# State read of blocks 2 to 7: softmax columns turned by VectorE in 32x32 squares and spread over partitions by DMA, with the division by the sum behind the read

## The chip, the cores and the metric

The kernel runs on one core of one Trainium2 chip. The metric is the device time of one execution in microseconds (us); the median of three runs of the kernel before is 890.83 us. A core has five engines with instruction queues of their own: TensorE (PE; its weight loads are listed as PEld), VectorE (DVE), ScalarE (ACT), GpSimd (POOL) and SyncE (SP), which here issues the DMAs.

## The reference, cut to what matters

Shapes: B = 8 blocks (batches), H = 8 heads, S = 512 tokens, NS = 32 states, D = 64. The change lies in the second softmax, which lets the states read from the tokens.

```python
scores = scale * x @ state.T                 # [B, H, S, NS]
xread  = softmax(scores) @ state             # tokens read from the states
scores2 = scale * state @ x.T                # [B, H, NS, S]
a2 = exp(scores2 - scores2.max(-1))
a2 /= a2.sum(-1) + 1e-9
sread = a2 @ x                               # states read from the tokens
y = concat([xread, sread], axis=2)           # 576 rows of width 512 per block
y = y + relu(layernorm(y) * g @ w_ch1) @ w_ch2
out = (sigmoid(causal_conv(y)) * (y @ w_val)) @ w_out
```

## The kernel before, in words

The eight blocks are worked one after the other by `segment`, which runs over sixteen pieces f of the hidden layer. One piece is, on PE, six matmuls of 512 columns into a PSUM bank `mm` (L77 to L79, `mm<-ahl,m`) and, one piece later, twelve matmuls of 512 columns that add the hidden piece into four banks `acc` (`acc<-hid,w`). Between them ACT (L680) and DVE (L684) take the hidden piece out of `mm`, of which there are two banks.

The attention of block b+1 is done in the background of block b: `background(b)` yields once per piece, and in it `attention_steps(b + 1)` does a step at each yield: scores (L213), the two softmaxes, the turning of the second softmax (`softmax2_turn`, L287), and three yields later the state read (`sread`, L304). PE's order is the order of the program; the order on the other engines and on SP's queue is set by a scheduler from priorities. Block 2 differs: its attention runs in the second half of block 1 (pieces 8 to 15, after two quiet yields), which has too few yields, so that what is left of its steps stands together at piece 15.

The second softmax has two tiles `a2[u]` of 128 rows (4 heads x 32 states) by 512 tokens. The read needs the tokens on the partitions. So in `softmax2_norm` ACT divides `a2` by its sum (L279, two instructions of 128x512), in `softmax2_turn` PE turns it (eight transposes of 128x128, L287, against the identity) into two PSUM tiles `at`, ACT copies these into SBUF (L291, two of 128x512), and in `sread` PE does 32 small matmuls (L304; each is two records in the trace, so 64) of a 128x32 piece against the tokens `xn`. DVE turns the result in 32x32 squares (L308, 128x128) and SP stores it by four DMAs into `x1d` (L310).

Tiles with the tag `t2` share six buffers of 128x512. SP's DMAs signal their end on eight semaphores, DMAHW0 to DMAHW7, in turn: a DMA is issued only when the one eight places before it has landed.

Of the kernel before, what the change touches and what calls it, by code (L numbers as in the profile page):

```python
# [14 lines left out]
AF = mybir.ActivationFunctionType  # L15
# [5 lines left out]
P = 128  # L21
B, H, S, NS, D = 8, 8, 512, 32, 64
DM = H * D
DFF = 4 * DM
KT = DM // P
# [19 lines left out]
def tile_kernel(ctx: ExitStack, tc: tile.TileContext, xT, xk, stT, sn, w1, w2, wval, wout, convw, gln, ident, out):  # L45
    nc = tc.nc
# [8 lines left out]
    def sb(shape, dt, tag, bufs=1):  # L55
        cnt[0] += 1
        return main.tile(shape, dt, tag=tag, bufs=BUFS.get(tag, bufs), name=f"{tag}_{cnt[0]}")

    def ps(pool, tag, shape):
        cnt[0] += 1  # L60
        return pool.tile(shape, F32, tag=tag, name=f"{tag}_{cnt[0]}")

    def at_ps(shape):
        return ps(ps_at, "at", shape)

    def t2(shape):
        return sb(shape, F32, "t2")

    def small(shape, dt, tag):
        return sb(shape, dt, tag, 2)  # L70
# [10 lines left out]
    def at_prio(p):  # L81
        tc.cur_priority = p
# [14 lines left out]
    def load_state(b, eng=nc.sync):  # L97
        st_raw = small([P, KT, NS], F32, "st_raw")
        eng.dma_start(out=st_raw, in_=stT[b])
        sn_raw = small([P, 2, D], F32, "sn_raw")  # L100
        eng.dma_start(out=sn_raw, in_=sn[b])
        loads[b] = [st_raw, sn_raw]

    def load_x(b, eng=nc.sync):
        xt = sb([P, KT, S], F32, "big")
        eng.dma_start(out=xt, in_=xT[b])
        loads[b].append(xt)

    def load_xk(b):
        xn = sb([P, 4, H, D], F32, "big")  # L110
        nc.sync.dma_start(out=xn, in_=xk[b])
        loads[b].append(xn)

    def state_coefs(b):
        st_raw, sn_raw = loads[b][:2]
        stg = small([P, KT, NS], F32, "stg")
        eng = nc.vector if b == 1 else nc.gpsimd
        a = eng.tensor_tensor(stg, st_raw, g_sb.to_broadcast([P, KT, NS]), op=ALU.mult)
        if b == 1:
            behind(a, "dve")  # L120
        sbn = small([P, 2, 1], F32, "sbn")
        a = nc.vector.tensor_reduce(sbn.rearrange("p u o -> p (u o)"), sn_raw, axis=AX.X, op=ALU.add)
        if b == 1:
            behind(a, "dve")
        nc.vector.tensor_scalar(sbn, sbn, -1.0 / DM, None, op0=ALU.mult)
        sbhl = small([P, 2, 2, 1], F32R, "sbhl")
        split_sb(sbhl[:, 0], sbhl[:, 1], sbn, eng)
        coef[b] = (stg, sn_raw, sbn, sbhl)
# [79 lines left out]
    def scores(b, sc):  # L208
        st_raw, _, xt = loads[b][:3]
        for p in range(KT):  # L210
            for u in range(2):
                r = slice(64 * u, 64 * u + 64)
                nc.tensor.matmul(sc[u][32 * p:32 * p + 32, :], lhsT=st_raw[r, p, :], rhs=xt[r, p, :], start=True, stop=True)  # L213
        e1 = []
        for u in range(2):
            e = t2([P, 16, NS])
            nc.vector.transpose(e.rearrange("p g n -> p (g n)"), sc[u])
            e1.append(e)
        att[b] = e1

    def softmax1_max(b):
        e1 = att[b]
        mx = sb([P, 2, 16, 1], F32, "mxden")
        for u in range(2):
            nc.vector.tensor_reduce(mx[:, u].rearrange("p g o -> p (g o)"), e1[u], axis=AX.X, op=ALU.max)
            nc.vector.tensor_tensor(e1[u], e1[u], mx[:, u].to_broadcast([P, 16, NS]), op=ALU.subtract)
            nc.scalar.activation(e1[u], e1[u], AF.Exp, scale=SCALE)

    def softmax1_norm(b):
        e1 = att[b]  # L230
        den = sb([P, 2, 16, 1], F32, "mxden")
        for u in range(2):
            nc.vector.tensor_reduce(den[:, u].rearrange("p g o -> p (g o)"), e1[u], axis=AX.X, op=ALU.add)
        dv = den.rearrange("p u g o -> p (u g o)")
        nc.vector.tensor_scalar(dv, dv, 1e-9, None, op0=ALU.add)
        nc.vector.reciprocal(dv, dv)
        for u in range(2):
            nc.vector.tensor_tensor(e1[u], e1[u], den[:, u].to_broadcast([P, 16, NS]), op=ALU.mult)
# [14 lines left out]
    def softmax1_out(b):  # L253
        softmax1_turn(b)
        softmax1_split(b)

    a2s = {}

    def softmax2_exp(b, sc):
        if b:  # L260
            a2 = [t2([P, S]) for _ in range(2)]
        else:
            a = sb([P, KT, S], F32, "x1")
            a2 = [a[:, u] for u in range(2)]
        nmax = small([P, 2], F32, "nmax")
        sum2 = small([P, 2], F32, "sum2")
        for u in range(2):
            nc.vector.tensor_reduce(nmax[:, u:u + 1], sc[u], axis=AX.X, op=ALU.max)
            nc.scalar.activation(nmax[:, u:u + 1], nmax[:, u:u + 1], AF.Copy, scale=-SCALE)
            nc.scalar.activation(a2[u], sc[u], AF.Exp, bias=nmax[:, u:u + 1], scale=SCALE, accum_out=sum2[:, u:u + 1])  # L270
        a2s[b] = (a2, sum2)

    def softmax2_norm(b):
        a2, sum2 = a2s[b]
        r2 = small([P, 2], F32, "r2")
        nc.vector.tensor_scalar(r2, sum2, 1e-9, None, op0=ALU.add)
        nc.vector.reciprocal(r2, r2)
        for u in range(2):
            nc.scalar.activation(a2[u], a2[u], AF.Copy, scale=r2[:, u:u + 1])  # L279

    def softmax2_turn(b):
        a2 = a2s[b][0]
        a2T = []
        for u in range(2):
            tp = at_ps([P, 4, P])
            for c in range(4):
                nc.tensor.transpose(tp[:, c, :], a2[u][:, c * P:(c + 1) * P], ident_sb)  # L287
            t = t2([P, 4, P])
            p = tc.cur_priority
            at_prio(p - HLEAD)  # L290
            nc.scalar.copy(t, tp)  # L291
            at_prio(p)
            a2T.append(t)
        a2s[b] = a2T

    def sread(b):
        a2T = a2s.pop(b)
        xn = loads[b][3]
        sr = ps(ps_mm, "mm", [P, 2, D]) if b > 1 else at_ps([P, 2, D])
        for u in range(2):  # L300
            for c in range(4):
                for p in range(KT):
                    r = slice(32 * p, 32 * p + 32)
                    nc.tensor.matmul(  # L304
                        sr[r, u, :], lhsT=a2T[u][:, c, r], rhs=xn[:, c, 2 * p + u, :], start=(c == 0), stop=(c == 3)
                    )
        srs = t2([P, 4, 32])
        nc.vector.transpose(srs.rearrange("p t n -> p (t n)"), sr.rearrange("p u d -> p (u d)"))  # L308
        for p in range(KT):
            nc.sync.dma_start(  # L310
                out=x1d[b, :, p, :].rearrange("(t j) n -> j t n", j=32), in_=srs[32 * p:32 * p + 32]
            )
# [43 lines left out]
    def mean_terms(b):  # L356
        sbn, aT = coef[b][2], aTs[b]
        t = t2([P, S])
        nc.scalar.activation(t, aT[:, 0], AF.Copy, scale=sbn[:, 0])
        nc.vector.scalar_tensor_tensor(t, aT[:, 1], sbn[:, 1], t, op0=ALU.mult, op1=ALU.add)  # L360
        terms[b] = halves_of(t, S)
# [71 lines left out]
    def attention_steps(b):  # L433
        state_coefs(b)
        sc = [at_ps([P, S]) for _ in range(2)]
        scores(b, sc)
        softmax2_exp(b, sc)
        yield
        softmax1_max(b)
        yield  # L440
        softmax2_norm(b)
        yield
        softmax1_norm(b)
        yield
        softmax2_turn(b)
        yield
        softmax1_out(b)
        mean_terms(b)
        yield
        yield  # L450
        sread(b)
        yield
        if b + 1 < B:
            load_state(b + 1)
            load_x(b + 1)
            load_xk(b + 1)
# [436 lines left out]
    def first():  # L893
        x1 = x1_steps(0)
        next(x1)
        yield
        next(x1)
        state_coefs(1)
        yield
        yield  # L900
        softmax1_split(0)
        next(x1)
        yield
        att1 = attention_start(1)
        next(att1)
        yield
        softmax2_norm(0)
        next(att1)
        yield
        next(att1)  # L910
        for _ in x1:
            pass
        softmax2_turn(0)
        yield
        sread(0)
        yield
# [166 lines left out]
```

## Time and profile before

| what | value |
|---|---|
| median of 3 runs | 890.83 us (890.58 to 890.91) |
| the profiled execution: its own time / its span | 890.99 us / 889.2 us |
| busy: PE / DVE / ACT / POOL | 873.5 / 571.8 / 385.8 / 210.3 us |
[...]
| PE matmuls of L287, blocks 1 to 7 (56) | 7.5 us busy |
| PE matmuls of L304, blocks 2 to 7 (384 records) | 6.6 us busy |

Busy time is a sum over an engine's instructions, merged where they overlap. The span is what the profiler saw from the first to the last instruction; the execution's own time holds 1.8 us more around it.

### The profile page before, as it was taken

Reading aid. Unit: us, or ns where it says so; the run is one execution under the profiler, and the core shown is the slowest. Engines: PE = TensorE matmul, PEld = TensorE weight load, DVE = VectorE, ACT = ScalarE, POOL = GpSimd, SP = SyncE. Lnnn points to the kernel's source line nnn. Section 1 sums busy time; section 2 is a strip of 40 time slices with the busy share of each in tenths; the row PEclk is TensorE's granted clock in tenths of the full one; section 3 lists DMA queues with packets and bytes.
Section 4 is the critical chain, followed back from the end, with each engine's and each line's share of the span. In section 5 each row is a group of like instructions: output and inputs, shape, how many; then the busy total and the mean of one; then the engine's idle time right before and its main releaser. Section 6 shows DMA issues by size and latency. Waiting matters only on the chain.

```text
span 889.2 us, 12522 instructions
## 1 busy us (share of the span) xinstructions
PE 873.5 (98%) x4970; PEld 666.0 (75%) x4970; DVE 571.8 (64%) x957; ACT 385.8 (43%) x715; POOL 210.3 (24%) x172
## 2 busy tenths in 40 slices
PE   7997999999999999999999999999999999999998
PEld 2355767777777777777777777777899988888886
DVE  6899985666644553573464446243468799988870
ACT  4865744243433341443443235132337555455531
POOL 0001010013234321513522442162301124322100
PEclk8999999999999999999999999999999999999999
DMA  9932210121112101211120100110130212222112
GB/s 358 408 109 74 98 52 1 74 73 53 51 48 76 54 0 52 74 51 52 51 71 1 63 36 1 27 48 1 48 139 6 95 71 77 90 96 95 69 73 72
DMA packets 26667, 66.44 MB, mean 75 GB/s; under 512 B 10864, under 2 KB 13040, under 8 KB 22512
## 3 DMA queue, kind: packets, MB, share of 16 engines
q1 hardware_dynamic: 25984, 65.24, 20.4%
q8 instruction: 39, 0.64, 0.3%
q10 hardware_dynamic: 624, 0.40, 0.2%
q14 instruction: 20, 0.16, 0.1%
HBM read 47.80 MB, written 17.83 MB: 74 GB/s over the span
## 4 chain that ended last, share of the span: by engine, by line
PE 92%; DVE 4%; DMA 2%; ACT 1%; issue 1%; SPq 0%; DVEq 0%; ACTq 0%
PE acc L77 16%; PE acc L78 16%; PE acc L79 16%; PE mm L77 9%; PE mm L78 9%; PE mm L79 9%; PE at L144 2%; PE at L77 2%; PE at L79 2%; PE at L78 2%; PE mm L144 1%; PE mm L982 1%; DMA big<-in_xT 1%; PE mm L651 1%; PE acc L697 1%; PE at L287 1%
## 5 line engine op out<-in xcount | busy, mean ns | idle before, releaser
L77 PE MATMUL acc<-hid,w 128*128 128x512 f32 (+1 forms) x560 | 212.3, 379 | 0.1
L78 PE MATMUL acc<-hid,w 128*128 128x512 f32 (+1 forms) x560 | 211.4, 378 | 0.0
L79 PE MATMUL acc<-hid,w 128*128 128x512 f32 (+1 forms) x560 | 211.3, 377 | 0.0
L684 DVE SCALAR_TENSOR_TENSOR hid<-mm,hid 128x512 fp32r<-128x512 f32 (+1 forms) x140 | 91.8, 655 | 159.5 <-ACT hid L680 159.4
L680 ACT ACTIVATE hid<-mm 128x512 fp32r<-128x512 f32 (+2 forms) x144 | 82.2, 571 | 205.5 <-PE mm L79 204.1
L77 PE MATMUL mm<-ahl,m 128*128 128x512 f32 (+1 forms) x312 | 119.7, 384 | 3.4 <-DVE ahl L249 1.7
L77 PEld LDWEIGHTS acc<-hid,w 128*128 128x128 f32 x560 | 105.4, 188 | 23.0 <-issue 1.7
L79 PEld LDWEIGHTS acc<-hid,w 128*128 128x128 f32 x560 | 105.4, 188 | 19.8
L78 PEld LDWEIGHTS acc<-hid,w 128*128 128x128 f32 x560 | 105.4, 188 | 19.5
L78 PE MATMUL mm<-ahl,m 128*128 128x512 f32 (+1 forms) x312 | 115.3, 369 | 1.2 <-DVE m L74 1.2
L79 PE MATMUL mm<-ahl,m 128*128 128x512 f32 (+1 forms) x312 | 115.0, 369 | 0.0
L763 DVE SCALAR_TENSOR_TENSOR ahl<-big,cw,ahl 128x511 f32<-128x511 f32 (+3 forms) x128 | 102.2, 843 | 0.3
L74 POOL TENSOR_TENSOR m<-mb,m 128x512 fp32r<-128x512 f32 x48 | 61.4, 1299 | 123.0 <-ACT m L73 123.0
L73 ACT ACTIVATE m<-mb 128x512 fp32r<-128x512 f32 x62 | 38.7, 632 | 110.7 <-DVE mb L155 110.5
L77 PEld LDWEIGHTS mm<-ahl,m 128*128 128x128 f32 x312 | 58.8, 188 | 36.7 <-issue 12.1
L78 PEld LDWEIGHTS mm<-ahl,m 128*128 128x128 f32 x312 | 58.9, 189 | 11.3 <-DVE m L74 2.4
L79 PEld LDWEIGHTS mm<-ahl,m 128*128 128x128 f32 x312 | 58.8, 189 | 9.9
L749 POOL TENSOR_TENSOR w<-big,w 128x512 fp32r<-128x512 f32 x24 | 38.1, 1617 | 92.8 <-ACT w L747 92.8
L78 PE MATMUL acc<-w,raw 128*128 128x512 f32 (+1 forms) x144 | 54.3, 377 | 0.0
L79 PE MATMUL acc<-w,raw 128*128 128x512 f32 (+1 forms) x144 | 54.3, 377 | 0.0
L77 PE MATMUL acc<-w,raw 128*128 128x512 f32 (+1 forms) x144 | 54.3, 377 | 0.0
L711 DVE TENSOR_TENSOR t<-acc,t 128x512 f32<-128x512 f32 (+1 forms) x44 | 28.0, 660 | 28.3 <-PE acc L79 28.2
(183 smaller groups left out, 1294.9 us busy)
## 6 DMA issues: line engine op xcount, KB each, us to landing
w<-in_w SPq DMA_DIRECT2D x20, 512.0 KB, 8.6
big<-in_xT SPq DMA_DIRECT2D x8, 1024.0 KB, 5.1
big<-in_xk SPq DMA_DIRECT2D x8, 1024.0 KB, 5.3
x2d<-x SPq DMA_DIRECT2D x8, 1024.0 KB, 4.0
big<-x2d SPq DMA_DIRECT2D x8, 1024.0 KB, 4.9
out<-hid SPq DMA_DIRECT2D x16, 512.0 KB, 2.8
raw<-in_w SPq DMA_DIRECT2D x12, 512.0 KB, 6.7
raw<-in_wval SPq DMA_DIRECT2D x4, 512.0 KB, 4.1
```

What stands on the lines that cost most here:

```text
L73: nc.scalar.activation(hi, src, AF.Copy)
L74: eng.tensor_tensor(lo, src, hi.bitcast(F32), op=ALU.subtract)
L77: nc.tensor.matmul(acc, lhsT=wh, rhs=xl, start=first, stop=False)
L78: nc.tensor.matmul(acc, lhsT=wl, rhs=xh, start=False, stop=False)
L79: nc.tensor.matmul(acc, lhsT=wh, rhs=xh, start=False, stop=last)
L144: nc.tensor.matmul(mp[u][32 * p:32 * p + 32, :], lhsT=stg[r, p, :], rhs=w1s[4 * q + p][r], start=True, stop=True)
L287: nc.tensor.transpose(tp[:, c, :], a2[u][:, c * P:(c + 1) * P], ident_sb)
L680: marks["act"] = nc.scalar.activation(hid[:, 0], h, AF.Relu)
L684: marks["dve"] = nc.vector.scalar_tensor_tensor(hid[:, 1], h, 0.0, hid[:, 0].bitcast(F32), op0=ALU.max, op1=ALU.subtract)
L711: marks["dve"] = nc.vector.tensor_tensor(t, accs[d], rrow, op=ALU.mult)
L749: nc.gpsimd.tensor_tensor(lo, src, hi.bitcast(F32), op=ALU.subtract)
L763: t = nc.vector.scalar_tensor_tensor(g[:, j:], x[:, :n - j], cw_sb[:, k, PAD - j:TAPS - j], g[:, j:], op0=ALU.mult, op1=ALU.add)
```

## The change

For blocks 2 to 7 `softmax2_turn` gives way to `softmax2_spread`. DVE turns each 32x32 square of `a2[u]` in place of the whole (`nc.vector.transpose`, one instruction of 128x512 for each u), and sixteen DMAs for each u (32 rows of 512 bytes, 16 KB) move the squares to the partitions that they belong to. The tokens come out in another order over the partitions; the host lays `xk` out to suit for these blocks. The division by the sum moves behind the read for all eight blocks: ACT scales the 128x64 results (two instructions) out of PSUM into a tile `read`, and DVE turns that one. Blocks 0 and 1 keep the transposes on PE.

```diff
@@ softmax2_norm
-        for u in range(2):
-            nc.scalar.activation(a2[u], a2[u], AF.Copy, scale=r2[:, u:u + 1])
+        r2s[b] = r2
@@ softmax2_turn
-            a2T.append(t)
+            a2T.append(t.rearrange("p c (k n) -> p c k n", n=32))
+        a2s[b] = a2T
+
+    def softmax2_spread(b):
+        a2 = a2s[b][0]
+        a2T = []
+        for u in range(2):
+            turned = t2([P, 4, P])
+            nc.vector.transpose(turned.rearrange("p q x -> p (q x)"), a2[u])
+            t = t2([P, 4, P])
+            for p in range(KT):
+                for q in range(4):
+                    nc.sync.dma_start(out=t[32 * q:32 * q + 32, p], in_=turned[32 * p:32 * p + 32, q])
+            a2T.append(t.rearrange("p k (c n) -> p c k n", n=32))
         a2s[b] = a2T
@@ sread
-                        sr[r, u, :], lhsT=a2T[u][:, c, r], rhs=xn[:, c, 2 * p + u, :], start=(c == 0), stop=(c == 3)
+                        sr[r, u, :], lhsT=a2T[u][:, c, p], rhs=xn[:, c, 2 * p + u, :], start=(c == 0), stop=(c == 3)
-        srs = t2([P, 4, 32])
-        nc.vector.transpose(srs.rearrange("p t n -> p (t n)"), sr.rearrange("p u d -> p (u d)"))
+        read, srs, r2 = t2([P, 2, D]), t2([P, 4, 32]), r2s.pop(b)
+        for u in range(2):
+            nc.scalar.activation(read[:, u], sr[:, u], AF.Copy, scale=r2[:, u:u + 1])
+        nc.vector.transpose(srs.rearrange("p t n -> p (t n)"), read.rearrange("p u d -> p (u d)"))
@@ attention_steps
-        softmax2_turn(b)
+        softmax2_spread(b)
@@ kernel (host layout)
+    xk = x.reshape(B, H, 4, P, D).transpose(0, 3, 2, 1, 4).copy()
+    xk[2:] = x[2:].reshape(B - 2, H, 4, 4, 32, D).transpose(0, 2, 4, 3, 1, 5).reshape(B - 2, P, 4, H, D)
```

The first place is PE at the end of block 1's pieces, where block 2's turn and read stand. In the kernel before, eight transposes and six matmuls stand ahead of the read:

```order
L79 MATMUL acc_297_1541<-hid_1681,w_13_243_1226 128x512
L287 MATMUL at_1725<-ident_78,t_307_1589 128x128 x4
L287 MATMUL at_1732<-ident_78,t_308_1590 128x128 x4
L77 MATMUL mm_1739<-ahl_642,m_1510 128x512
L78 MATMUL mm_1739<-ahl_642,m_1510 128x512
L79 MATMUL mm_1739<-ahl_642,m_1510 128x512
L77 MATMUL mm_1739<-ahl_642,m_1510 128x512
L78 MATMUL mm_1739<-ahl_642,m_1510 128x512
L79 MATMUL mm_1739<-ahl_642,m_1510 128x512
L304 MATMUL mm_1761<-big_1178,t_328_1730 32x64 x16
L304 MATMUL mm_1761<-big_1178,t_330_1737 32x64 x16
```

In the changed kernel the transposes are gone from this row and the rest stands as it did. In blocks 3 to 7, too, only the transposes leave PE's order; there 54 matmuls of other work stand between turn and read.

The second place is VectorE ahead of block 2's read, behind the maxima of the first softmax (L225); here the changed kernel's row:

```order
L225 TENSOR_REDUCE mxden_1623<-t_308_1589 128x16
L698 SCALAR_TENSOR_TENSOR hid_1608<-mm_1601,hid_1608 128x512
L300 STREAM_TRANSPOSE t_329_1725<-t_309_1591 128x512
L226 TENSOR_TENSOR t_307_1587<-t_307_1587,mxden_1623 128x512
L226 TENSOR_TENSOR t_308_1589<-t_308_1589,mxden_1623 128x512
L276 TENSOR_SCALAR r_318_1652<-sum_312_1594 128x2
L300 STREAM_TRANSPOSE t_331_1744<-t_310_1592 128x512
L698 SCALAR_TENSOR_TENSOR hid_1637<-mm_1630,hid_1637 128x512
```

The two transposes (L300; L698 is the old L684) are new, before and behind the subtractions of L226; the scheduler has put them as soon as their exponentials are there, well ahead of where the step stands in the program. Blocks 3 to 7 have the same row. On SP's queue the 32 DMAs of block 2 then stand so:

```order
L730 DMA x2d_69<-x_71_328 128x2048
L106 DMA big_1831<-in_xT 128x2048
L99 DMA st_raw_2445<-in_stT 128x128
L304 DMA t_330_1727<-t_329_1725 32x128 x16
L304 DMA t_332_1746<-t_331_1744 32x128 x16
L111 DMA big_1833<-in_xk 128x2048
L324 DMA x1d<-t_341_1819 32x4x32 x4
```

They lie between the loads of the next block's `xT` and state and the load of its `xk`, which in both kernels waits for the read.

The third place is the read itself on PE in block 4, with the semaphores that each matmul waits for; the changed kernel's row:

```order
L316 MATMUL mm_3020<-big_2451,t_530_2903 32x64 [waits DMAHW3_49,DMAHW2_49,DMAHW6_49,DMAHW1_49,DMAHW0_49]
L316 MATMUL mm_3020<-big_2451,t_530_2903 32x64 [waits DMAHW6_49,DMAHW7_49,DMAHW5_49,DMAHW4_49]
L316 MATMUL mm_3020<-big_2451,t_530_2903 32x64 [waits DMAHW2_49,DMAHW3_49,DMAHW1_49,DMAHW0_49]
L316 MATMUL mm_3020<-big_2451,t_530_2903 32x64 [waits DMAHW6_49,DMAHW7_49,DMAHW5_49,DMAHW4_49]
L316 MATMUL mm_3020<-big_2451,t_530_2903 32x64 x12
L316 MATMUL mm_3020<-big_2451,t_532_2922 32x64 [waits DMAHW2_49,DMAHW3_49,DMAHW1_49,DMAHW0_49]
L316 MATMUL mm_3020<-big_2451,t_532_2922 32x64 [waits DMAHW6_49,DMAHW7_49,DMAHW5_49,DMAHW4_49]
L316 MATMUL mm_3020<-big_2451,t_532_2922 32x64 [waits DMAHW2_49,DMAHW3_49,DMAHW1_49,DMAHW0_49]
L316 MATMUL mm_3020<-big_2451,t_532_2922 32x64 [waits DMAHW6_49,DMAHW7_49,DMAHW5_49,DMAHW4_49]
L316 MATMUL mm_3020<-big_2451,t_532_2922 32x64 x12
```

The first four matmuls of each half u each wait for the four DMAs that filled their piece. Waits beyond what a matmul carries itself are instructions of their own on PE's queue: the built program has 16 of them in each read of blocks 3 to 7 and 17 in that of block 2, where the kernel before had at most one.

## Rows read from the trace of the kernel before

**Rows 1.** The page: busy time of each engine, share of the span, instructions.
```profile
PE 873.5 (98%) x4970; PEld 666.0 (75%) x4970; DVE 571.8 (64%) x957; ACT 385.8 (43%) x715; POOL 210.3 (24%) x172
```

**Rows 2.** The page: the chain that ended last, by engine.
```profile
PE 92%; DVE 4%; DMA 2%; ACT 1%; issue 1%; SPq 0%; DVEq 0%; ACTq 0%
```

**Rows 3.** Busy time by stretch: span; PE, PEld, DVE, ACT, POOL; clock; DMA.
```profile
236.00:274.00 38.00, 38.00 (x253) 29.73 (x253) 17.38 (x30) 12.72 (x24) 7.39 (x7) 1.00 0.10 30
```

**Rows 4.** PE's timeline (start, us, what), block 3's turn.
```profile
247.58 1.09 PE L287 MATMUL at<-ident,t 128*128 128x128 f32 x8
248.57 0.50 PE L77 MATMUL mm<-ahl,m 128*128 128x512 f32 x1
```

**Rows 5.** PE's timeline, block 2's turn and read.
```profile
192.07 0.39 PE L79 MATMUL acc<-hid,w 128*128 128x512 f32 x1
192.30 1.04 PE L287 MATMUL at<-ident,t 128*128 128x128 f32 x8
193.09 0.48 PE L77 MATMUL mm<-ahl,m 128*128 128x512 f32 x1
...
194.64 1.10 PE L304 MATMUL mm<-big,t 128*32 128x64 f32 x64
```

**Rows 6.** PE's timeline, block 3's read.
```profile
261.04 1.10 PE L304 MATMUL mm<-big,t 128*32 128x64 f32 x64
262.07 1.09 PE L144 MATMUL at<-w,stg 64*32 64x512 f32 x16
263.09 0.50 PE L77 MATMUL mm<-ahl,m 128*128 128x512 f32 x1
```

**Rows 7.** Line L304: durations in ns (min/median/max), first and last start.
```profile
L304 PE MATMUL mm<-big,t x384: 219/219/243, 194.6 to 563.7; 128*32 128x64 f32 x192
...
L304 PEldq EVENT_SEMAPHORE  x3: 51/51/51, 66.6 to 191.4; - x3
```

**Rows 8.** DVE's timeline in blocks 2 and 3; brackets: idle before, its releaser.
```profile
178.91 1.28 DVE L226 TENSOR_TENSOR t<-t,mxden 128x512 f32<-128x512 f32 x2
...
234.07 0.68 DVE L684 SCALAR_TENSOR_TENSOR hid<-mm,hid 128x512 fp32r<-128x512 f32 x1
...
262.21 0.32 DVE L308 STREAM_TRANSPOSE t<-mm 128x128 f32<-128x128 f32 x1 [2.46 <-PE mm L304]
```

**Rows 9.** DVE's groups: count, busy us, mean ns, idle before.
```profile
L243 DVE STREAM_TRANSPOSE aT<-t 128x512 f32<-128x512 f32 x16 | 10.5, 687 | 0.0
```

**Rows 10.** ACT's groups, likewise.
```profile
L279 ACT ACTIVATE t<-t,r 128x512 f32<-128x512 f32 x14 | 9.3, 711 | 0.0
L291 ACT COPY t<-at 128x512 f32<-128x512 f32 x16 | 9.0, 575 | 2.5 <-PE at L287 2.5
...
L680 ACT ACTIVATE hid<-mm 128x256 fp32r<-128x256 f32 x16 | 6.1, 379 | 18.3 <-PE mm L79 18.2
```

**Rows 11.** ACT's timeline behind block 3's read.
```profile
264.04 1.23 ACT L73 ACTIVATE m<-mb 128x512 fp32r<-128x512 f32 x2 [5.02 <-DVE mb L155]
```

**Rows 12.** SP's timeline: DMA issues of blocks 2, 4 and 7.
```profile
175.20 0.38 SPq L99 DMA_DIRECT2D st_raw<-in_stT  x1
...
338.06 1.81 SPq L310 DMA_DIRECT2D x1d<-t  x4
...
564.32 2.02 SPq L310 DMA_DIRECT2D x1d<-t  x4
```

**Rows 13.** Line L310, the 16 KB stores: issue in ns, landing in us.
```profile
L310 SPq DMA_DIRECT2D x1d<-t x32: 303/424/1631, 73.8 to 565.9; - x32
...
DMA to landing us min/median/max: 1.5/3.9/5.8
```

**Rows 14.** DMA issues of block 7's stores alone: KB, us to landing.
```profile
x1d<-t SPq DMA_DIRECT2D x4, 16.0 KB, 1.7
```

**Rows 15.** The chain that ended last, in block 0's turn: start, us, what.
```profile
65.88 0.65 DVE mb L155
66.53 0.60 DVE c L523
```

More of the change, by code (lines that the diff above doesn't have):

```diff
@@ L255, in softmax1_out @@
         softmax1_split(b)
-    a2s = {}
+    a2s, r2s = {}, {}
     def softmax2_exp(b, sc):
@@ L1059 @@
         "xT": x.reshape(B, KT, 2, S, D).transpose(0, 2, 4, 1, 3).reshape(B, P, KT, S),
-        "xk": x.reshape(B, H, 4, P, D).transpose(0, 3, 2, 1, 4),
+        "xk": xk,
         "stT": state.reshape(B, KT, 2, NS, D).transpose(0, 2, 4, 1, 3).reshape(B, P, KT, NS),
```

## The prediction

> **What bounds the kernel now.** I read the page first: PE is busy for 98% of the span [rows 1], and 92% of the chain that ended last lies on PE [rows 2]. The stretch that holds block 3's turn and read says the same from nearer: of 38 us, PE has 38.0, VectorE 17.4, ScalarE 12.7, at full granted clock and with the DMA engines a tenth busy [rows 3]. So what is taken from VectorE or ScalarE is worth nothing by itself, nor does adding to them cost anything while their results come in time. What counts is PE's time, and waits that open on PE. I then went to PE's timeline at the turn and the read, to the engines that feed them, and to SP's issues, since the change puts 192 DMAs there.
>
> **What it removes from PE.** In block 3 the eight transposes take from 247.58 to the start of the next L77 at 248.57, 0.99 us [rows 4]. Blocks 3 to 7 look alike, so five times 0.99 is 4.95. Block 2's take from 192.30 to 193.09, 0.79 [rows 5]. Together −5.74 us. (The table's 7.5 us for 56 such matmuls is busy time, which counts the overlap with neighbours; I take the starts.)
>
> **What it moves on ScalarE and VectorE.** ScalarE loses two divisions of 0.711 and two copies of 0.575 us in a block, 2.6 us, and gains two of 128x64. No row has that shape; 128x256 takes 0.379 [rows 10], and I estimate 0.23 for a quarter of the division's width. VectorE gains two transposes of 128x512, 0.687 each [rows 9], 1.4 us in a block. Both engines have over half of the 38 us free [rows 3], so I cost this at nothing. What could spoil it is the PSUM bank: VectorE released the read's bank at 262.21 + 0.32 = 262.53 [rows 8]; now ScalarE does, some 0.46 us behind the read's end at about 262.2, at 262.7. If the next L77 at 263.09 [rows 6] needs that bank, 0.4 us is still free, and ScalarE idles there (5.02 us before 264.04) [rows 11]. Without that idle time it would be up to 0.7 us (a division's length) in a block; I take 0. In blocks 0 and 1, where only the division moves, the chain runs over VectorE while ScalarE divides (65.88 to 67.1) [rows 15], so nothing is gained there; at most the two divisions, 1.4 us.
>
> **When the spread is done.** A DMA takes SP 424 ns to issue (303 to 1631) and lands 1.5 to 5.8 us after, median 3.9 [rows 13]. Four of them in a row take 1.81 us (0.45 apart) in block 4 and 2.02 in block 7 [rows 12]. The 3.9 is that of stores queued right behind a load of 1 MB; block 7's, which have none ahead, landed in 1.7 [rows 14], and the spread has none close ahead, so it is nearest to those. These go to DRAM, the new ones from SBUF to SBUF, which no row shows. I take 0.46 apart and 1.7 to land: 31 × 0.46 + 1.7 = 16.0 us from the first issue to the last landing. The bounds are 31 × 0.35 + 1.5 = 12.4 (0.35 an estimate inside the issue's 303 to 424 ns) and 31 × 0.53 + 3.9 = 20.3.
>
> In block 3 the last exponential's neighbour on VectorE, L684 at 234.07, ends at 234.75 [rows 8]; with a transpose behind it the first DMA goes at about 235.4 and the last lands at 251.4, at the latest bound 255.7. The read is due at 261.04 [rows 6] less the 0.99, at 260.05. So 8.6 us are free, and the wait costs nothing in blocks 3 to 7 unless issues come (24.6 − 1.7)/31 = 0.74 us apart. Behind the spread on SP stand the load of the next tokens and the stores, which wait for the read anyway.
>
> Block 2 has no such room. Its first transpose takes the place of the subtraction at 178.91 [rows 8] and ends at 179.6; SP has been free since 175.58 [rows 12]. The second ends before SP is through the first sixteen. The last landing is at 179.6 + 16.0 = 195.6 (192.0 to 199.9). The read starts at 194.64 [rows 5], less 0.79, and its second half, whose DMAs are last, half a microsecond later: 194.36. PE then waits 1.2 us, and nothing else can go, since its order is fixed; the bounds are 0 and 5.5. Six matmuls and the turn are all that lay between turn and read here.
>
> **What it adds on PE.** Each read has 16 wait instructions (17 in block 2). One takes 51 ns [rows 7], and they belong to PE's queue, which runs ahead of the matmuls: the one at 191.4 is for the read at 194.64 [rows 5, 7], 3.2 us ahead, that is 3 + 8 + 6 = 17 matmuls. The first eight waits, 0.41 us, lie ahead of a read with 512-column matmuls of 0.23 us before it, and are covered. The other eight stand behind 16 of the read's matmuls, which go at 1.03 us / 64 = 16 ns a record [rows 6]; a lead of 17 of these is 0.27 us, so 0.41 − 0.27 = 0.14 is exposed. Some of the first eight may show as well; I take 0.25 a read, 1.5 in all, between 0 (the lead covers all) and 16 × 0.051 = 0.82 a read, 4.9 in all.
>
> The trace's lead is 17 matmuls with their weight loads, 34 instructions. [...]
>
> **The sum.** −5.74 + 1.5 + 1.2 = −3.0 us. From the profiled execution's 890.99 that is 888.0. It ran 0.16 above the median of 890.83, which is within what I can tell.
>
> **Rivals.** *Full gain.* The waits are covered, SP issues at 0.35, and block 2 waits for nothing: 890.99 − 5.74 = 885.2. For it speaks the lead of 3.2 us, against it the short matmuls inside the read.
>
> *A wash.* All wait instructions show, since the queue's lead shrinks in the read: −5.74 + 4.9 + 1.2 = +0.4, 891.4. For it: the waits stand amid the shortest matmuls of the kernel. Against it: the first eight follow long ones.
>
> *Slower, by SP's pace.* If a DMA lands only after 5.8 us, as the slowest store did [rows 13], then, as each waits for the one eight places before, they go 5.8/8 = 0.73 apart, and the spread takes 31 × 0.73 + 5.8 = 28.4 us. Block 2's read then waits until 208.0, 13.6 us, and the five others until 263.8, 3.7 us each: −5.74 + 1.5 + 13.6 + 18.5 = +27.9, 918.9. It decides where block 2's wait is over 6.0 us, from (200.4 − 179.6 − 1.7)/31 = 0.62 apart on. At 0.7 block 2 alone waits 9 us, and the time is about 896. Against it: the landing of 1.7 without a load ahead, and 0.45 to 0.5 between issues. For it: thirty-two in a row are more than any row of before shows.
>
> [...]
>
> **How the numbers follow.** Some 0.2%, 1.8 us, is what a measurement of this kernel can tell from no change: faster is below 889.0, slower above 892.6. I give the forecast (886.4 to 889.0) 0.48, the full gain 0.16, the wash and what lies beside it (889.0 to 892.6) 0.25, and SP's pace 0.11. Faster is 0.48 + 0.16 = 0.64, same 0.25, slower 0.11. The range goes from the full gain, 885.2, to 892.2, the wash with a wait in block 2 of 2 us: it leaves out SP's pace and little more.
>
> **What would show it.** No L287 in blocks 2 to 7, and each L77 behind L144 1 us earlier in its block. SP's 32 issues some 0.46 apart, over by 251 in block 3; PE without a gap at the reads of blocks 3 to 7, and the read there 1.0 to 1.8 us from start to the next matmul (1.03 is covered waits, over 1.5 is the wash). In block 2 a gap of about 1 us between the halves of the read, ended by a DMA. I am wrong if that gap is over 6 us, if the reads of blocks 3 to 7 wait for DMAs, or if PE waits for ScalarE's two new instructions behind them.

## The result, and the profile after

The changed kernel takes 902.38 us (median of 6 runs, 901.8 to 906.88) where the kernel before takes 890.87: 1.0135 times as long, interval 1.0113 to 1.0156. The forecast was 888.0 with a range to 892.2. It became slower by 11.5 us, and on the side of the rival that was given 0.11, SP's pace, though that accounts for only part of it. In the profiled executions of seven of the experiments below PE's clock falls for a while at about 85 us (granted clock 0.72 or 0.73 over 82 to 88 us, against 1.00 in the others and in the two kernels compared here), which costs each of them some 1.6 us between 81 and 95 us, so differences of that size are read from starts behind that place and not from medians.

The page of the changed kernel, PE's share, the chain that ended last by engine, and the DMAs of the spread (KB each, us to landing). Compare [rows 1, 2].

```profile
PE 874.0 (97%) x4921; PEld 664.4 (74%) x4922; DVE 577.3 (64%) x969; ACT 376.0 (42%) x703; POOL 209.3 (23%) x172
...
PE 88%; DVE 5%; DMA 3%; SPq 1%; ACT 1%; issue 1%; DVEq 0%; ACTq 0%
...
t<-t SPq DMA_DIRECT2D x192, 16.0 KB, 1.8
```

The span grew by 10.8 us, to 900.0, and PE's busy time by 0.5: PE waits. To find where, I set the start of the same matmul in the two executions beside each other and followed the difference along the program:

| place (start before, start after) | ahead or behind (us) | step |
|---|---|---|
| block 1, piece 15 (L78): 189.80, 189.34 | −0.46 | the program up to here |
| L77 behind block 2's turn: 193.09, 191.88 | −1.21 | −0.75: the turn is gone |
| L77 behind block 2's read: 195.67, 202.25 | +6.58 | +7.79: the read waits |
| L78 of the next piece: 198.75, 206.41 | +7.66 | +1.08: lower clock |
| L77 behind block 3's turn: 248.57, 256.24 | +7.67 | +0.01, for a turn of 0.99 taken out |
| L144 behind block 3's read: 262.07, 270.36 | +8.29 | +0.62: the read itself |
| L144 behind block 7's read: 563.83, 574.66 | +10.83 | +2.54: four more reads, and nothing for four turns |

Three things make up the loss: block 2's read (8.9 us with the clock behind it), the reads of blocks 3 to 7 (3.0 us: 1.61 to 1.67 each for 1.03), and five turns that gave nothing (the forecast counted on 4.95).

A fourth loss is small and stands just ahead of the table's first row. In the kernels that spread block 2, VectorE's L698, which takes the hidden piece out of `mm`, comes later, and the weight load of the next L77 waits for it:

```profile
189.01 0.19 PEld L77 LDWEIGHTS acc<-hid,w 128*128 128x128 f32 x1 [0.51 <-DVE hid L698]
```

PE loses some 0.25 us there in each of them, and nothing in e4 and e6, where PE turns block 2. The two transposes are the work on VectorE that is new there (0.70 us each, from 178.09 and 179.95); no run shows them by themselves.

**Block 2's read.** PE's timeline; in brackets the idle time before an entry and what ended it. Before, it was one row of 64 records [rows 5].

```profile
193.33 0.65 PE L316 MATMUL mm<-big,t 128*32 128x64 f32 x32
194.35 0.30 PE L316 MATMUL mm<-big,t 128*32 128x64 f32 x2 [0.37 <-DMA t<-t]
196.22 0.27 PE L316 MATMUL mm<-big,t 128*32 128x64 f32 x2 [1.57 <-DMA t<-t]
198.67 0.42 PE L316 MATMUL mm<-big,t 128*32 128x64 f32 x2 [2.18 <-DMA t<-t]
201.29 1.03 PE L316 MATMUL mm<-big,t 128*32 128x64 f32 x26 [2.20 <-DMA t<-t]
202.25 0.79 PE L77 MATMUL acc<-hid,w 128*128 128x512 f32 x1
```

The second half waits four times for a DMA, once for each group of four, some 2.5 us apart. SP's timeline and the line of the spread (issue in ns, then landing in us) say why:

```profile
178.82 21.12 SPq L304 DMA_DIRECT2D t<-t  x32
...
243.09 20.83 SPq L304 DMA_DIRECT2D t<-t  x32
```

```profile
L304 SPq DMA_DIRECT2D t<-t x192: 507/589/1483, 178.8 to 568.2; - x192
...
DMA to landing us min/median/max: 1.7/1.8/3.5
```

An issue takes 589 ns, and the 32 take 21 us: they start 0.63 us apart from the first pair on, with one issue of 1.48 us among them, where the stores of [rows 12] went 0.45 to 0.5 apart. The landing, 1.8 us, is as forecast. Nothing stands between the issues that they could wait for: eight of them span over 5 us, the landing takes 1.8.

**The clock behind it.** Busy time by stretch (us; PE, PEld, DVE, ACT, POOL; granted clock; DMA). From 194.4 to 201.3 PE is busy for 0.96 of 6.9 us (0.53 and 0.43 in the first two rows). Inside that wait the granted clock falls: it is 0.96 on average up to 198 and 0.50 from there. It is back at about 204.5; until then the matmuls behind the read start 0.43 us apart and not 0.23:

```profile
194.40:198.00 3.60, 0.53 (x4) 0.23 (x4) 0.42 (x1) 0.00 (x0) 0.00 (x0) 0.96 0.09 24
198.00:201.30 3.30, 0.43 (x4) 0.22 (x5) 0.00 (x0) 0.00 (x0) 0.00 (x0) 0.50 0.10 25
...
202.30:204.30 2.00, 2.00 (x6) 1.61 (x6) 1.02 (x2) 0.52 (x2) 0.00 (x0) 0.50 0.46 70
204.30:206.00 1.70, 1.70 (x9) 1.34 (x8) 0.00 (x0) 0.00 (x0) 0.00 (x0) 0.93 0.99 410
```

**The place of block 3's turn.** PE and VectorE; before, the eight transposes stood where PE now idles [rows 4].

```profile
254.23 1.09 PE L144 MATMUL mm<-w,stg 64*32 64x512 f32 x16
255.44 1.41 DVE L155 SCALAR_TENSOR_TENSOR mb<-cs,sbn,mm 128x512 f32<-128x512 f32 x2 [1.77 <-PE mm L144]
...
256.24 0.50 PE L77 MATMUL mm<-ahl,m 128*128 128x512 f32 x1 [0.92 <-DVE mb L155]
```

Ahead of the turn, L144 fills both PSUM banks of `mm`, and the next hidden piece (L77) needs one of them. VectorE's L155 frees it, and L77 starts when the first L155 is through (255.44 and half of 1.41 is 256.15). In the kernel before the bank came free just as late, and the transposes ran inside that time. In its trace L155 stands at the same distance behind L144 (1.21 us):

```profile
247.77 1.41 DVE L155 SCALAR_TENSOR_TENSOR mb<-cs,sbn,mm 128x512 f32<-128x512 f32 x2 [2.44 <-PE mm L144]
```

The view of waits (us in total, times, longest) counts how often the weight load of L77 waited for L155, here before and then after:

```profile
PEld mm L77 <- DVE mb L155: 7.0, 6, 2.5
```

The six of the kernel before lie at other places, and none at a turn. One is at 84.2; the other five, 0.9 us each, stand where another L144 fills `mm` and the scores (L213) run on PE in the meantime (at 230.0 for block 3). In the changed kernel the five turns come to these, 1.8 us each:

```profile
PEld mm L77 <- DVE mb L155: 16.1, 11, 2.5
```

**The read of blocks 3 to 7.** PE's timeline in block 3, and the wait instructions of this line in the stretches 264 to 266.1 and 268.7 to 270.4 (count: ns min/median/max, first and last start). Compare [rows 6, 7].

```profile
268.72 1.71 PE L316 MATMUL mm<-big,t 128*32 128x64 f32 x64
270.36 1.09 PE L144 MATMUL at<-w,stg 64*32 64x512 f32 x16
```

```profile
L316 PEldq EVENT_SEMAPHORE  x8: 51/51/51, 264.6 to 266.0; - x8
...
L316 PEldq EVENT_SEMAPHORE  x8: 51/51/51, 268.9 to 269.7; - x8
```

The DMAs have landed before this read is due (the last issue ends at 263.9), so it waits for none; it takes 1.64 us and not 1.03. The first eight wait instructions begin 4.1 us ahead of the read and end before it; the other eight stand inside it, where their starts span 0.8 us.

### The profile page after: what moved, and what is told of

It reads as the page before. It is cut to its first block, busy times and chain, and to the rows that moved or that the text cites. A ratio compares the mean times of both kernels' runs of the same rounds, so it can differ in the third digit from the quotient of the medians.

```text
span 900.0 us, 12822 instructions
## 1 busy us (share of the span) xinstructions
PE 874.0 (97%) x4921; PEld 664.4 (74%) x4922; DVE 577.3 (64%) x969; ACT 376.0 (42%) x703; POOL 209.3 (23%) x172
## 4 chain that ended last, share of the span: by engine, by line
PE 88%; DVE 5%; DMA 3%; SPq 1%; ACT 1%; issue 1%; DVEq 0%; ACTq 0%
PE acc L77 16%; PE acc L78 16%; PE acc L79 16%; PE mm L77 9%; PE mm L78 8%; PE mm L79 8%; PE at L144 2%; PE at L77 2%; PE at L79 2%; PE at L78 2%; PE mm L144 1%; SPq L304 1%; DMA raw<-in_w 1%; PE mm L316 1%; DVE mb L155 1%; PE mm L665 1%
## 5 line engine op out<-in xcount | busy, mean ns | idle before, releaser
L77 PE MATMUL acc<-hid,w 128*128 128x512 f32 (+1 forms) x560 | 213.0, 380 | 0.2
L78 PE MATMUL acc<-hid,w 128*128 128x512 f32 (+1 forms) x560 | 211.8, 378 | 0.0
L698 DVE SCALAR_TENSOR_TENSOR hid<-mm,hid 128x512 fp32r<-128x512 f32 (+1 forms) x140 | 91.9, 657 | 162.7 <-ACT hid L694 162.6
L77 PE MATMUL mm<-ahl,m 128*128 128x512 f32 (+1 forms) x312 | 119.6, 383 | 8.4 <-DVE mb L155 6.2
L77 PEld LDWEIGHTS acc<-hid,w 128*128 128x128 f32 x560 | 105.6, 189 | 23.6 <-issue 1.8
L78 PEld LDWEIGHTS acc<-hid,w 128*128 128x128 f32 x560 | 105.7, 189 | 19.6
L78 PE MATMUL mm<-ahl,m 128*128 128x512 f32 (+1 forms) x312 | 115.2, 369 | 0.4 <-DVE m L74 0.4
L77 PEld LDWEIGHTS mm<-ahl,m 128*128 128x128 f32 x312 | 58.8, 188 | 45.5 <-DVE mb L155 16.1
L78 PEld LDWEIGHTS mm<-ahl,m 128*128 128x128 f32 x312 | 58.9, 189 | 10.6 <-DVE m L74 1.8
L78 PE MATMUL acc<-w,raw 128*128 128x512 f32 (+1 forms) x144 | 54.3, 377 | 0.0
L77 PE MATMUL acc<-w,raw 128*128 128x512 f32 (+1 forms) x144 | 54.3, 377 | 0.0
```

The lines of the kernel that those rows point to most:

```text
L77: nc.tensor.matmul(acc, lhsT=wh, rhs=xl, start=first, stop=False)
L78: nc.tensor.matmul(acc, lhsT=wl, rhs=xh, start=False, stop=False)
L698: marks["dve"] = nc.vector.scalar_tensor_tensor(hid[:, 1], h, 0.0, hid[:, 0].bitcast(F32), op0=ALU.max, op1=ALU.subtract)
```

## The experiments

### The turn taken out alone: e1_no_turn, e2_no_turn_at

```diff
     def softmax2_turn(b):
         a2 = a2s[b][0]
+        if b > 1:
+            a2s[b] = [a.rearrange("p (c x) -> p c x", c=4) for a in a2]
+            return
@@ segment, in e2_no_turn_at only
-                m_steps(*unit, "mm")
+                m_steps(*unit, "at" if f == 9 else "mm")
```

> The kernel before with the turn of blocks 2 to 7 left out altogether (no transposes, no copies; the read takes the untransposed softmax, so its numbers mean nothing). Theory 1: in blocks 3 to 7 the turn's 0.99 us lies over a wait of PE for VectorE's L155, which frees the PSUM bank that the next L77 needs; taken out, PE idles about 0.9 us there and only block 2's 0.75 us is won: about 890 us. Rival (the prediction's term): 5.74 us are won, about 885.2 us.

> As e1_no_turn, and the eighth-tile group L144 that stands ahead of the turn (piece 9 of blocks 2 to 6) writes into the two at banks that the turn used, not into the two mm banks. Theory 1: with the mm banks free the next L77 starts at once, so the whole turn is won: 0.75 + 5 x 0.92 = 5.3 us, about 885.5 us. Rival: the bank has no part in it, and the time is that of e1_no_turn.

e1 took 890.53 us, 0.9993 of the kernel before (0.9983 to 1.0002): 48 transposes taken out, and no gain that stands clear of the noise. e2 took 886.08, 0.9934 (0.992 to 0.9947). PE at block 3's turn in e1, and then in e2:

```profile
247.80 1.09 PE L144 MATMUL mm<-w,stg 64*32 64x512 f32 x16
...
249.82 0.50 PE L77 MATMUL mm<-ahl,m 128*128 128x512 f32 x1 [0.93 <-DVE mb L155]
```

```profile
247.56 1.09 PE L144 MATMUL at<-w,stg 64*32 64x512 f32 x16
248.58 0.50 PE L77 MATMUL mm<-ahl,m 128*128 128x512 f32 x1
```

From L144 to L77 takes 2.02 us in e1, as with the transposes between them (2.01 from 246.56 to 248.57 in the kernel before), and 1.02 in e2. Followed along the program, e2 wins 1.0 us at each of the five places, e1 nothing at any; both win 0.8 at block 2's. So the turn's price is 1 us a block, and the bank decides whether it is paid.

### The bank without the rest: e10_before_at

The same line of `segment` in the kernel before, the turn left on PE.

> The kernel before with the group L144 of piece 9 in the at banks (all else as before, the turn on PE too). Theory: VectorE's L155 must free a bank in any case before PE goes on; before, the turn ran in that time. Here the turn itself needs the at banks and waits for L155, so the time is paid in full: 0.9 us more in each of five blocks, 891.2 + 4.6 = 895.8 us. Rival: the at banks are the better place whatever the turn does, and this alone gives the gain of e2_no_turn_at and e7_dram_at: about 886.5 us.

896.54 us, 1.0045 (1.0028 to 1.0062). The turn now needs the banks that L155 frees, and the wait stands ahead of it:

```profile
249.15 1.31 PE L287 MATMUL at<-ident,t 128*128 128x128 f32 x8 [0.92 <-DVE mb L155]
```

Each of the five places loses 1.1 us. The `at` banks are worth something only where the turn has left them.

### The changed kernel with that bank: e3_at

> The changed kernel, with the group L144 of piece 9 (blocks 2 to 6) in the two at banks instead of the two mm banks. Theory: the 0.92 us that PE idles for L155 at the place of the old turn go in five blocks, and nothing else: 902.4 - 4.6 = 897.8 us. Rival: that idle time is only moved, to the reads, which then wait for their last DMAs (they would be due some 1 us before now, and land some 3 us ahead of it): no gain, 902.4 us.

898.28 us (897.19 to 898.88), 4.1 below the changed kernel; the five places win 1.0 us each (block 3's L77 starts 1.02 us behind its L144), and the reads behind them do not wait for their DMAs though they are due earlier.

### Block 2 back on PE: e4_pe2

```diff
-        softmax2_spread(b)
+        (softmax2_turn if b == 2 else softmax2_spread)(b)
```

(and the old layout of the tokens for block 2.)

> The changed kernel with block 2 alone turned by PE as before. Theory: block 2's read loses its 7.9 us of waiting for the DMAs and the 1.0 us at the lower clock behind it, and pays the turn's 0.75 us again: 902.4 - 8.2 = 894.2 us, where blocks 3 to 7 still read 0.6 us longer each. Rival: the wait comes back at block 3, whose DMAs are also issued 0.63 us apart: above 896 us.

894.25 us, 1.0026 (1.0017 to 1.0036), 8.1 us below the changed kernel. Block 2's read is one row of 64 records again, and block 3's takes as long as in the changed kernel without a wait for a DMA:

```profile
198.38 1.10 PE L316 MATMUL mm<-big,t 128*32 128x64 f32 x64
...
264.81 1.68 PE L316 MATMUL mm<-big,t 128*32 128x64 f32 x64
```

### What an issue costs: e8_four, e5_dram

```diff
@@ e8_four
-            for p in range(KT):
-                for q in range(4):
-                    nc.sync.dma_start(out=t[32 * q:32 * q + 32, p], in_=turned[32 * p:32 * p + 32, q])
+            for q in range(4):
+                nc.sync.dma_start(out=t[32 * q:32 * q + 32], in_=turned[32 * q:32 * q + 32])
@@ e5_dram
+            for p in range(KT):
+                nc.sync.dma_start(
+                    out=a2d[b, u][:, p].rearrange("(q j) x -> j q x", j=32), in_=turned[u][32 * p:32 * p + 32]
+                )
+        for u in range(2):
+            t = t2([P, 4, P])
+            nc.sync.dma_start(out=t, in_=a2d[b, u])
```

> The changed kernel with four DMAs for each half in place of sixteen: each moves 32 rows of 2 KB from SBUF to SBUF onto the same partitions, so the squares are not spread (that part is left out). It measures what SP pays for an issue: if it pays for the DMA, 0.6 us each, 8 x 0.63 + 2 = 7 us for the block; if for the bytes or pieces, 2.4 us each and 21 us as now. By the first block 2's wait goes and the reads keep four waits a half: about 892 us; by the second 900 us.

> The changed kernel with the squares spread by way of DRAM: for each half four stores of 64 KB (32 rows, four pieces of 512 bytes) and one load of 256 KB, ten DMAs in a block for 32, and one or two semaphores for the read to wait on for 16 waits. Theory: block 2's 7.9 us of waiting, the 1.0 us at the lower clock and the 3.1 us of wait instructions in the reads of blocks 3 to 7 all go: 902.4 - 12.0 = 890.4 us, each read 1.03 us. Rivals: the trip through DRAM takes longer than the 15 us that block 2 has, so that its wait stays (898 us); or the reads are slow for another reason than their waits, and 893.5 us are left.

e8 took 890.41 us in its one run, e5 890.85, 0.9995 of the kernel before (0.9986 to 1.0005). SP and block 3's read in e8, then in e5:

```profile
179.54 5.03 SPq L303 DMA_DIRECT2D t<-t  x8
...
260.45 1.10 PE L315 MATMUL mm<-big,t 128*32 128x64 f32 x64
```

```profile
179.39 3.73 SPq L303 DMA_DIRECT2D a2d<-t  x8
183.31 1.55 SPq L308 DMA_DIRECT2D t<-a2d  x2
...
193.88 1.10 PE L320 MATMUL mm<-big,t 128*32 128x64 f32 x64
...
260.28 1.10 PE L320 MATMUL mm<-big,t 128*32 128x64 f32 x64
```

Eight DMAs of 64 KB take 5.03 us to issue, 0.63 each, as those of 16 KB do: between these two sizes, from SBUF to SBUF, SP pays for the DMA and not for its bytes. The stores of the same size to DRAM take 0.47 each. Why the route makes that difference no run shows. By way of DRAM the block's ten DMAs are issued by 184.9, and block 2 waits for nothing. In e5 the reads of all six blocks take 1.03 us. The trip through DRAM keeps all of the change's other parts, so nothing else in the change was dear.

### What the wait instructions cost: e9_collect, e11_collect

In e9 GpSimd touched the spread tiles in place, but its trace has as many wait instructions at this line as the changed kernel's, 99, so the edit did not do what it was for; its reads of blocks 3 to 7 took 1.60 to 1.74 us (904.16 us). e11 gives the second half a tile of its own:

```diff
+        if b > 2:
+            fresh[b] = f = sb([P, 3, P], F32, "fresh")
+            nc.gpsimd.tensor_scalar(f, flat_of.pop(b)[:, 1:], 1.0, None, op0=ALU.mult)
@@ sread
+                    w = fresh[b][:, p - 1, 32 * c:32 * c + 32] if b in fresh and u and p else a2T[u][:, c, p]
```

> The changed kernel, where in blocks 3 to 7 GpSimd multiplies the two spread tiles by one in place before the read, so that PE waits for GpSimd alone and not for 32 DMAs: the same DMAs, the wait instructions gone from PE. Theory: each of these five reads takes 1.03 us again, 0.63 less: 902.4 - 3.1 = 899.3 us. Rival: the reads are long because their operands have only just landed or lie otherwise, not for the wait instructions: no change, 902.4 us.

> As e9_collect was meant to be, for the second half alone: in blocks 3 to 7 GpSimd copies three quarters of its spread tile into a tile of its own before the read, so that of this half's eight wait instructions two stay on PE; the DMAs and the first half's eight are as in the changed kernel. Theory: the first half's are gone through ahead of the read, the second half's are what shows, so these five reads take 1.03 to 1.1 us instead of 1.63 to 1.7: 3.0 us less, 899.4 us. Rival: the reads are long for another reason, and nothing changes: 902.4 us, reads of 1.7 us.

901.24 us (899.61 to 902.18). The medians say little here, since the profiled execution had the low clock at the start that the changed kernel's had not: granted 0.73 over 82 to 88 us, and 2.6 us behind the changed kernel at 123 us. Behind that the five reads win it all back: block 7's L144 behind the read starts at

```profile
574.58 1.09 PE L144 MATMUL at<-w,stg 64*32 64x512 f32 x16
```

for 574.66 in the changed kernel. Each read takes 1.03 us (block 3's from 271.55 to 272.58), with the first half's eight wait instructions still there and two of the second half's.

### The division alone, and the parts together: e6_div, e7_dram_at

> Only the division moved behind the read, for all blocks; the turn stays on PE everywhere, no spread. Theory: ScalarE and VectorE have room, PE's work is the same, and what is won is the 0.5 us by which the changed kernel was ahead before block 2's read: about 890.4 us. Rival: two more ScalarE instructions behind the read hold the read's PSUM bank so that PE waits up to 0.5 us in a block: 893 us.

> e5_dram and e3_at together. Theory: both gains add: 890.4 - 4.6 = 885.8 us, below the kernel before by about 5 us.

e6 took 891.59 us, 0.9997 (0.9988 to 1.0006): the division's move costs and gives nothing that can be measured, which rules out the rival's 2 us. Inside block 0 it does give something: in every kernel with the division moved, the L78 that starts at 49.49 in the kernel before waits 0.8 us less for `m`. Here the kernel before, and then e6:

```profile
49.49 0.50 PE L78 MATMUL mm<-ahl,m 128*128 128x512 f32 x1 [0.97 <-DVE m L74]
```

```profile
47.77 0.50 PE L78 MATMUL mm<-ahl,m 128*128 128x512 f32 x1 [0.16 <-DVE m L74]
```

In e1, e2 and e10, which keep the division where it was, this wait stays. The gain does not last: at the matmul that starts at 121.76 in the kernel before, the kernels with the division moved fall back by 0.35 to 1.3 us, and e1, e2 and e10 by at most 0.3. The changed kernel's −0.46 at 189.80 is made mainly of these two steps (−0.8 and +0.35), of the wait for L698 (+0.25, above), and of 0.43 that this execution was ahead by 20 us already, where those of the experiments lie between −1.3 and +0.35. e7 took 887.05 (885.75 to 887.26), 0.9947 (0.9931 to 0.9964): the version that beats both. It wins 0.8 us at block 2's turn and 1.0 at each of the five others.

## Why the prediction was wrong

Between the forecast's −3.0 us and the measured +10.8 of the two spans lie 13.8. Of these the turns of blocks 3 to 7 make 5.0, block 2's read with the clock behind it 7.7 (8.9 for 1.2) and the reads of blocks 3 to 7 another 1.5; some 0.4 the other way is the program ahead of them.

**The removed transposes: "so five times 0.99 is 4.95".** This step failed for blocks 3 to 7; for block 2 it was right (0.75 measured, 0.79 forecast). 0.99 us from the turn to the next L77 is what the turn took, not what taking it out gives. L77 needed a bank that VectorE frees some 0.9 us after L144, and PE stands still for that time when nothing else fills it. e1, e2 and e10 show it from three sides. It could have been read beforehand: L155 ends its first instruction where L77 starts (247.77 and half of 1.41, 248.48, and 248.57 [rows 4]), and at the scores of the same blocks the weight load's wait for L155 stands in the view of waits. The place behind the read [rows 6], where L77 follows L144 by 1.02 us, misled: there L144 writes `at`.

**SP's pace: "I take 0.46 apart".** The nearest row was of stores to DRAM; from SBUF to SBUF an issue costs 0.63. With that the forecast's own sum gives 31 × 0.63 + 1.8 = 21.3 us from 178.82, 200.2, and one issue of 1.48 us makes it 201; the read's last wait ended at 201.29. The rival named 0.62 as the pace from which block 2 decides, but it gave slow landings as the cause, and these were not slow. For blocks 3 to 7 the 8.6 us of room were enough, as forecast. In the runs 64 KB cost SP the same 0.63 as 16 (e8), and e5, with ten DMAs in place of 32 and fewer waits, is 11.5 us below the changed kernel.

**The clock behind the wait.** Not foreseen: in 6.9 us of little work on PE (0.96 us busy) the granted clock fell from 1.00 to 0.50, and it stayed there until about 204.5, another 1.08 us behind the read.

**The wait instructions: "so 0.41 − 0.27 = 0.14 is exposed".** The mechanism was right, the term mis-sized: 0.6 a read and not 0.25, 3.0 in all for 1.5, inside the bounds of 0 and 4.9. The second eight are not 0.41 us long: they start 0.11 to 0.14 us apart, and from the first start to the end of the last they span 0.89; less the 0.27 of lead that the prediction reckoned, which is an estimate, that leaves 0.62. The first eight were hidden, as forecast: e11 keeps them and reads in 1.03. In block 3 the first wait begins 4.1 us ahead of the read, which is 18 matmuls of 0.23 us, and the lead is gone inside the read.

**ScalarE and the bank behind the read** cost nothing, as forecast (e6; behind block 3's read L77 follows L144 by 1.02 us in both kernels). The two instructions of 128x64 take 0.52 us for the 0.46 estimated; their 64 columns are an eighth of the division's 512, and not a quarter. VectorE's new work was also put at nothing, and ahead of block 2's read PE lost 0.25 us by the wait for L698. That nothing is gained in block 0 was wrong at one place: 0.8 us is won there, and 0.35 lost again at about 122 us.

Put together from the runs: −0.46 (up to 189.80) − 0.75 (block 2's turn) + 7.79 + 1.08 (its read and the clock) + 3.0 (the other reads) = 10.7, against 10.8 between the last matmuls of the two executions.

## What to carry to other kernels

Before counting an instruction's time on the busiest engine as gain, ask what the next instruction there waits for, and when that comes: here the end of L155 just where L77 starts was the sign, and at places of the same form the weight load's wait in the view of waits. Price a run of DMAs by a row of the same route (SBUF to SBUF here), and multiply the pace by their number before believing that they are hidden. Waits on many semaphores were hidden here ahead of long matmuls (0.23 us apart) and cost 0.6 us a read among short ones (64 records in 1.03 us); fewer, larger DMAs cured both SP's pace and the waits (e5: ten in a block, issued in 5.5 us, and reads of 1.03 us).

## What the runs showed of the hardware that was not expected

SP takes 0.63 us to issue a DMA from SBUF to SBUF, for 16 KB and for 64 KB alike, 0.47 us for a store of 64 KB to DRAM, both from 32 partitions. Wait instructions of 51 ns on PE's queue start 0.12 us apart on average among short matmuls (eight starts in 0.84 us). PE's granted clock went from 1.00 to 0.50 at about 197.7 us, inside a wait in which PE had been busy for 0.53 us since 194.4, and came back at about 204.5, behind some 3 us of full work.
